# A tensor-product message kernel for a graph: three parts of the edges become two, and the other operand of the summing matmul becomes stationary

## The chip, the core and the metric

The kernel runs on one core of a Trainium2 chip. The core has five engines that each run their own list of instructions in order: TensorE (PE in the profile; its loads of the stationary operand are listed as PEld), VectorE (DVE), ScalarE (ACT), GpSimd (POOL) and SyncE (SP). Engines wait for each other through semaphores. Transfers are issued here by SP and, where rows are gathered or scattered by index, by POOL. The metric is the time of one execution in microseconds (us) on the device; lower is better.

## The reference

There are 10,000 nodes and 640,000 edges; each node has 64 channels of 4 components. What must be computed:

```python
R   = silu(edge_feat @ w_rad)                     # (E, 64): one factor per edge and channel
xs  = x[src]                                      # (E, 64, 4): gather by source node
tp  = einsum('eci,ef,ifo->eco', xs, Y, cg)        # Y: (E, 4), cg: (4, 4, 4)
msg = R[:, :, None] * tp
agg = segment_sum(msg, dst, N)                    # sum over edges by destination node
out = einsum('ncm,cd->ndm', agg, w_mix)           # (N, 64, 4)
```

`src` and `dst` are random, so edges come in no order.

## The kernel before

Because `cg` and `w_mix` are constants, the kernel sums, for every node, the products R * x[src] times each of the four components of Y, and applies `cg` and `w_mix` once per node at the end (`mix`). The sum over edges is a matmul over tiles of 128 edges, for which the edges must first stand together by destination. So the work has three kinds of steps.

**The first pass** (`pass1`) reads the edges of one part and sorts them into 18 groups of 576 destination nodes. An edge is a payload of 9 words (a key of source and destination, 4 of Y, 4 of edge_feat). It works in chunks of 12 tiles: `tables` counts and lays out up to 24 chunks at a time (NC is 24 in the lead-in, 14 later), `route` then builds, per chunk, a one-hot matrix (`oh`, L546 on DVE, L552 and L553 on ACT) and a spread payload (`X`, L537 on DVE), multiplies them (`pr`, L560), copies the result out (`rt`, L567 on ACT) and stores it by index (L571, POOL) to the tensor `grp`.

**The second pass** (`pass2`) does the same with one group after the other, in chunks of 11 tiles, and sorts a group into its 18 buckets of 32 nodes (tensor `bkt`). It loads the group's words into `Wt2` (L704; two buffers, the next group's load issued while the present group is laid out), and at the end loads the sorted payload back as `pay` (L732).

**The messages** (`messages`) run over units. A unit is one bucket of one part: 5 tiles in the first part, 6 in the second and in the third. For a unit POOL gathers the rows x[src] (L790, one indirect transfer per tile, `LG` = 6 units ahead, 8 buffers of `xg`); PE transposes the payload (L803); ACT copies it (L808); PE forms the radial product (`pre`, L813); ACT applies SiLU (L816); DVE builds the one-hot of the destination times Y (`spots`, L824 and L827, tile `S`), and multiplies x[src] by R in place (`products`, L834). Then `sums` (L844) adds up, per tile, one matmul with S as the stationary operand (128 edges x 128 columns: 32 nodes by 4) and the product as the moving one (256 columns), so that the bucket's sum stands with its nodes on the partitions. Each fp32 matmul shows in the profile as two passes.

The parts are not kept apart on the chip: a bucket's sum of the first part goes to the DRAM tensor `sums` (L868), the second part fetches it (L855, tile `old`), adds it on DVE while it takes the sum out of PSUM (L864) and stores it again, and the third does the same without storing. For the third, `flip` (L879) transposes the sum on PE, since `mix` (L903) needs the channels on the partitions, and `flipped` (L887, ACT) takes it out. The sums live in one PSUM bank of two halves, which are taken in turn by `sums` and by `flip`.

**Order.** The lead-in runs `pass1` of the first part while the DRAM tensors are cleared; there only SP's order is written by hand. Afterwards `groups` writes the order of PE, DVE and ACT by hand: one step in four of each unit (`quarters`) is followed by as many steps of the other generators as their due times ask for. `pass1` of a later part is spread so that it ends before the second-to-last group of the part ahead of it is through; `pass2` of a group is spread over the units of the group ahead of it. So while the first part's 313 units run, the second part is sorted for the first time; while the second part's 313 units run, the third; and while the third part's units run only the second pass is left beside them.

A few lines that a sentence can't say:

```python
SPLIT = ((0.3, (5,)), (0.355, (6,)), (0.345, (6,)))      # share of the edges, tiles of each unit of a bucket
quarters = (((index, LI), (gather, LG), (fetch, 4), (turn, 2), (sums, 0), (flip, -1), (silu, 1)),
            ((turned, 2), (spots, 1)), ((products, 1), (evict, 0), (flipped, -1)), ((radial, 2), (full, -1)))
```

`(f, a)` means that in step k the stage `f` of unit k + a is issued.

Of the kernel before, what the change touches and what calls it, by code (L numbers as in the profile page):

```python
# [18 lines left out]
F = mybir.dt.float32  # L19
# [6 lines left out]
P = 128  # L26
B = 18
W = 9
# [7 lines left out]
SPLIT = ((0.3, (5,)), (0.355, (6,)), (0.345, (6,)))  # L36
LG = 6
# [34 lines left out]
class Kernel:  # L72
    def __init__(self, ctx, tc, x, src, dst, Y, ef, w_rad, cg, w_mix, out):
# [56 lines left out]
        self.sums = self.dr.tile([self.NBK, NB * 4, 256], F, name="sums")  # L130
# [11 lines left out]
    def consts(self):  # L142
        nc, c = self.nc, self.cst

        def iota(name, pat, base=0, cm=0):
            t = c.tile([P] + [n for _, n in pat], F, name=name)
            nc.gpsimd.iota(t, pattern=pat, base=base, channel_multiplier=cm,
                           allow_small_or_imprecise_dtypes=True)
            return t

        self.zr = c.tile([16, max(self.p1.rw, self.p2.rw)], F, name="zr")
        nc.vector.memset(self.zr, 0.0)
# [10 lines left out]
        d = iota("dif", [[1, P]], cm=-1)  # L163
# [17 lines left out]
        self.L = c.tile([P, P], F, name="L")  # L181
        nc.vector.tensor_scalar(self.L, d, -0.5, None, op0=OP.is_le)
# [64 lines left out]
    def weights(self):  # L247
# [23 lines left out]
        wm2 = self.ph.tile([P, 2, 64], F, name="wm2", bufs=1)  # L271
# [10 lines left out]

        m = self.ph.tile([P, 4], F, name="io", bufs=1)
        nc.gpsimd.iota(m, pattern=[[-1, 4]], base=P, channel_multiplier=1, allow_small_or_imprecise_dtypes=True)
        mi = self.ph.tile([P, 4], I32, name="ioi", bufs=1)
        nc.vector.tensor_copy(mi, m)
        nc.vector.tensor_scalar(mi, mi, 3, None, op0=OP.bitwise_and)
        nc.vector.tensor_scalar(m, mi, 0.0, None, op0=OP.is_equal)
        self.wx = c.tile([P, 2, 64, 4], F, name="wx")
        for h in range(2):  # L290
            nc.vector.tensor_tensor(self.wx[:, h], wm2[:, h, :].unsqueeze(2).to_broadcast([P, 64, 4]),
                                    m.unsqueeze(1).to_broadcast([P, 64, 4]), op=OP.mult)
# [313 lines left out]
    def pass1(self, part, first):  # L606
# [12 lines left out]
        TB, DB, KB, SB = {}, {}, {}, {}  # L619
        nc.vector.memset(self.k1, 0.0)  # L620

        def front(b):

            o, e = cut[b] * T, min(cut[b + 1] * T, nt)
            m = e - o
            da = ph.tile([P, NC * T], I32, name="da", bufs=1)
            si = SB[b] = ph.tile([P, NC * T], I32, name="si", bufs=2)
            nc.sync.dma_start(da[:, :m], self.dst[:, lo + o:lo + e])
# [509 lines left out]
```

## Time and profile before

| | us |
|---|---|
| median of 3 runs (10965.9 to 10981.9) | 10973.87 |
| the profiled execution | 10891.28 |
| its span, from first to last instruction | 10889.4 |
| PE, PEld busy | 8139.3, 6372.5 |
| DVE busy | 6985.1 |
| POOL busy | 6023.7 |
| ACT busy | 4132.0 |
| mean granted TensorE clock | 0.833 |

The profile describes one execution. Busy times are by engine; a row of a group of instructions gives source line, engine, operation, output<-inputs, the count, the busy time in us and the mean duration of one in ns, and after a second bar the idle time of the engine just ahead of such instructions with what ended it ("issue" is idle time for which the profile shows no wait). A row of stretches gives start:end, length, the busy time of each engine with its count of instructions in brackets, the granted TensorE clock, the share of the DMA engines and GB/s. An engine at 75% is not necessarily the bound, and one at 64% is not necessarily free: the four engines hand each unit to one another several times.

### The profile page before, as it was taken

To read this page: it belongs to the slowest core of one execution; us is meant where nothing else is said; L and a number is where in the kernel's file an instruction comes from. 1 tells how busy PE (TensorE), PEld (TensorE's weight loads), DVE (VectorE), ACT (ScalarE), POOL (GpSimd) and SP (SyncE) were. 2 spreads that over 40 slices of the span, in tenths; PEclk is the share of its full clock that TensorE was granted. 3 is DMA by queue.
4 is the path that set the end of the run, shared out by engine and by line. 5 is a ranking of instruction groups with operands and counts; after the bars stand their busy time and mean duration, and the time that the engine had idled before them with its cause. 6 is when DMAs were issued, how large, how long until landed. Compare 5 with 4: busy or idle time off the path is not lost. (4 is left out here: it accounts for less than half of the span.)

```text
span 10889.4 us, 127350 instructions
## 1 busy us (share of the span) xinstructions
PE 8139.3 (75%) x41365; PEld 6372.5 (59%) x41365; DVE 6985.1 (64%) x12762; ACT 4132.0 (38%) x12102; POOL 6023.7 (55%) x6306
## 2 busy tenths in 40 slices
PE   5767777777777777777777777776778787777876
PEld 5656566656565565556555555555556565655654
DVE  6777667777666676666666666656656565555553
ACT  5654444444444343334334333332323232333321
POOL 1225555555555655555655555566666666666664
PEclk8878888888888887788888887887888888888887
DMA  8213233333333323333333333333333333333332
GB/s 156 77 42 93 83 87 96 90 91 93 92 86 90 101 83 97 102 96 101 109 101 98 106 102 95 99 109 110 106 103 100 104 99 104 99 103 100 101 103 73
DMA packets 696241, 1056.05 MB, mean 97 GB/s; under 512 B 251979, under 2 KB 500327, under 8 KB 695576
## 3 DMA queue, kind: packets, MB, share of 16 engines
q0 software_dynamic: 286560, 746.72, 24.0%
q1 hardware_dynamic: 406424, 293.41, 10.1%
q8 instruction: 328, 5.37, 0.2%
q10 hardware_dynamic: 2592, 7.78, 0.2%
q14 instruction: 337, 2.76, 0.1%
HBM read 856.49 MB, written 207.52 MB: 98 GB/s over the span
## 5 line engine op out<-in xcount | busy, mean ns | idle before, releaser
L790 POOL DMA_INDIRECT xg<-in_x_dram,sidx x5321 | 5052.4, 950 | 3151.5 <-issue 1427.6
L560 PE MATMUL pr<-X,oh 128*128 128x135 f32 (+1 forms) x21286 | 3147.2, 308 | 674.4 <-ACT rt L567 294.3
L560 PEld LDWEIGHTS pr<-X,oh 128*128 128x128 f32 x21286 | 2971.7, 218 | 1021.9 <-issue 505.5
L844 PE MATMUL G<-xg,S 128*128 128x256 f32 x10642 | 2958.3, 430 | 408.4 <-issue 265.2
L844 PEld LDWEIGHTS G<-xg,S 128*128 128x128 f32 x10642 | 2250.4, 219 | 829.2 <-issue 321.7
L537 DVE TENSOR_TENSOR X<-dv,Wt 128x1512 f32<-128x1512 f32 (+4 forms) x958 | 1600.8, 1671 | 774.5 <-remote 482.0
L834 DVE TENSOR_TENSOR xg<-xg,pre 128x1536 f32<-128x1536 f32 (+1 forms) x939 | 1556.9, 1658 | 501.3 <-ACT pre L816 365.6
L552 ACT ACTIVATE sq<-i,rowf 128x128 f32<-128x128 f32 x5658 | 1750.0, 392 | 9.5 <-DVE rowf L524 7.2
L813 PE MATMUL pre<-wr,sT 54*128 54x384 f32 (+1 forms) x1878 | 942.9, 585 | 419.4 <-ACT sT L808 370.1
L864 DVE TENSOR_TENSOR Gp<-old,G 128x256 f32<-128x256 f32 x626 | 262.3, 419 | 1541.1 <-remote 710.6
L553 ACT ACTIVATE oh<-sq,ones 128x768 f32<-128x768 f32 (+2 forms) x958 | 937.1, 978 | 204.6 <-remote 98.0
L571 POOL DMA_INDIRECT grp<-rt,idx x417 | 415.6, 997 | 948.9 <-ACT rt L567 508.8
L571 POOL DMA_INDIRECT bkt<-rt,idx x541 | 541.3, 1001 | 670.6 <-ACT rt L567 411.8
L827 DVE TENSOR_TENSOR S<-dv,pay 128x768 f32<-128x768 f32 (+1 forms) x939 | 857.5, 913 | 82.8 <-PE G L844 23.1
L816 ACT ACTIVATE pre<-pre 128x384 f32<-128x384 f32 (+1 forms) x939 | 429.1, 457 | 1222.8 <-PE pre L813 349.3
L546 DVE TENSOR_TENSOR oh<-dv,rowf 128x640 f32<-128x640 f32 (+2 forms) x922 | 800.7, 868 | 1.2 <-remote 1.2
L567 ACT ACTIVATE rt<-pr 128x135 f32<-128x135 f32 (+1 forms) x958 | 259.5, 271 | 1114.9 <-remote 620.5
L813 PEld LDWEIGHTS pre<-wr,sT 54*128 54x128 f32 (+1 forms) x1878 | 312.4, 207 | 623.9 <-ACT sT L808 417.1
L808 ACT ACTIVATE sT<-pre 54x128 f32<-54x128 f32 (+1 forms) x939 | 244.6, 261 | 698.2 <-remote 362.8
L507 ACT ACTIVATE pc<-pp 128x396 f32<-128x396 f32 (+3 forms) x506 | 244.0, 482 | 507.7 <-PE pp L499 218.4
L887 ACT ACTIVATE Gs<-G 128x256 f32<-128x256 f32 x313 | 118.9, 380 | 830.4 <-DVE Gp L864 590.9
L903 PE MATMUL po<-wf,Gs 128*128 128x256 f32 (+2 forms) x1392 | 338.5, 399 | 78.4 <-ACT Gs L887 63.7
(216 smaller groups left out, 5316.2 us busy)
## 6 DMA issues: line engine op xcount, KB each, us to landing
xg<-in_x_dram,sidx POOLq DMA_INDIRECT x5321
sums<-Gp SPq DMA_DIRECT2D x626, 128.0 KB
old<-sums SPq DMA_DIRECT2D x626, 128.0 KB
bkt<-z SPq DMA_DIRECT2D x24, 994.5 KB
pay<-bkt SPq DMA_DIRECT2D x34, 486.0 KB
ys<-in_Y_dram SPq DMA_DIRECT2D x104, 96.0 KB
es<-in_edge_feat_dram SPq DMA_DIRECT2D x104, 96.0 KB
out_dram<-ot SPq DMA_DIRECT2D x69, 128.0 KB
```

The lines of the kernel that those rows point to most:

```text
L537: nc.vector.tensor_tensor(X[:, :m, :].rearrange("p t (s w) -> p t s w", w=W), msk.unsqueeze(3).to_broadcast([P, m, ps.r, W]), QD[c // Q][1 ...
L546: nc.vector.tensor_tensor(oh[:, :v, :], self.v128.unsqueeze(1).to_broadcast([P, v, P]), row[:, o:o + v].unsqueeze(2).to_broadcast([P, v, P ...
L552: nc.scalar.activation(sq[:, u, :], self.i128, AF.Square, bias=to, scale=-1.0)
L553: nc.scalar.activation(oh[:, v:v + len(at), :], sq[:, :len(at), :], AF.Relu, bias=self.ones[:, 0:1], scale=-2.0)
L560: nc.tensor.matmul(pr[:, :ps.rw], oh[:, u, :], X[:, u, :], start=(u == 0), stop=(not on and u == m - 1))
L571: st = nc.gpsimd.indirect_dma_start(out=ps.dst, out_offset=bass.IndirectOffsetOnAxis(ap=idx[:, i:i + 1], axis=0), in_=RT.pop(c), in_offset ...
L790: nc.gpsimd.indirect_dma_start(out=xg[:, t, :], out_offset=None, in_=self.x, in_offset=bass.IndirectOffsetOnAxis(ap=si[:, u:u + 1], axis=0))
L813: nc.tensor.matmul(R, ST_.pop(k)[:ut * W], self.wr[:ut * W, :ut * 64], start=True, stop=True)
L816: nc.scalar.activation(RT[k], RT[k], AF.Silu)
L827: nc.vector.tensor_tensor(S[:, :ut], self.eq[:, :ut].unsqueeze(3).to_broadcast([P, ut, NB, 4]), pb[:, :, 1:5].unsqueeze(2).to_broadcast([P ...
L834: nc.vector.tensor_tensor(V, V, R.unsqueeze(3).to_broadcast([P, ut, 64, 4]), op=OP.mult)
L844: nc.tensor.matmul(G, S[:, t].rearrange("p n f -> p (n f)"), V[:, t].rearrange("p c i -> p (c i)"), start=(s + t == 0), stop=(last(k) and ...
```

## The change

The edges are cut into two parts instead of three: 30% with units of 5 tiles as before, and 70% with two units of 6 tiles for every bucket. The numbers that follow from the code: groups of the second part have 224 tiles (before 115 and 112 in the two parts that it replaces); chunks of the first pass stay 417 (124 + 293 instead of 124 + 148 + 145); chunks of the second pass become 523 (157 + 366) instead of 541 (157 + 192 + 192); units stay 939 and tiles 5,321. All 293 chunks of the second part's first pass now run beside the first part's 313 units, and beside the other 626 units runs the second pass alone. `tables` in the second pass lays out up to 21 chunks at once, not 11.

Further edits in the same change:

- `sums` takes the product R * x[src] as the stationary operand, in two halves of 128 columns, and S as the moving one: per tile two matmuls of 128 columns instead of one of 256. The sum then already has the channels on the partitions; `flip` and `flipped` go, and the last part's sum is written straight into the tile that `mix` reads.
- The sum of a bucket has one PSUM buffer, with no second half.
- A bucket of the second part is taken out of PSUM once in two units; `sums` is stored and fetched 313 times each instead of 626.
- The second pass has one `Wt2`, loaded when the group ahead is through, six steps ahead of its use.
- Gathers run 5 units ahead (6 buffers of `xg`) instead of 6 (8 buffers); `old` is fetched 3 units ahead with 3 buffers; `didx` has one buffer.
- In the lead-in, the destinations and sources of the next table are loaded when the present table starts (they were loaded when their own table started), and Y and edge_feat are loaded three blocks ahead instead of two. `weights` comes after the first 40 steps of the first pass. While the first group goes through the second pass ahead of the first unit, the first pass of the second part is stepped along with it.
- The constants that only the overflow code at the end needs (`wx`, `zr`, `L`) are built there.

```diff
-SPLIT = ((0.3, (5,)), (0.355, (6,)), (0.345, (6,)))
-LG = 6
+SPLIT = ((0.3, (5,)), (0.7, (6, 6)))
+LG = 5
...
+        def ends(b):
+            if b >= nb:
+                return
+            o, e = cut[b] * T, min(cut[b + 1] * T, nt)
+            da = AB[b] = ph.tile([P, NC * T], I32, name="da", bufs=1 + self.early)
+            si = SB[b] = ph.tile([P, NC * T], I32, name="si", bufs=2 + self.early)
+            nc.sync.dma_start(da[:, :e - o], self.dst[:, lo + o:lo + e])
+            nc.sync.dma_start(si[:, :e - o], self.src[:, lo + o:lo + e])
...
+            if b == 0 or not self.early:
+                ends(b)
             if b == 0:
-                load(0)
-                load(1)
+                for i in range(self.ahead):
+                    load(i)
+            if self.early:
+                ends(b + 1)
...
-            Wt = ph.tile([P, M, W], F, name="Wt2")
+            Wt = ph.tile([P, M, W], F, name="Wt2", bufs=1)
...
+        for k, g in self.segs:
+            nt = self.gt[k][g]
+            Wt = load(k, g)
+
+            for _ in range(6):
+                yield
...
-            nxt = load(*self.segs[i + 1]) if i + 1 < len(self.segs) and self.segs[i + 1][0] == k else None
...
-            xg = XG[k] = ph.tile([P, UT, 256], F, name="xg", bufs=LG + 2)
+            xg = XG[k] = ph.tile([P, UT, 256], F, name="xg", bufs=LG + 1)
...
             if s == 0:
-                GP[g, j] = half()
+                GP[g, j] = self.ps.tile([P, 2, NB, 4], F, name="G", tag="G", bufs=1)
...
             for t in range(ut):
-                nc.tensor.matmul(G, S[:, t].rearrange("p n f -> p (n f)"), V[:, t].rearrange("p c i -> p (c i)"),
-                                 start=(s + t == 0), stop=(last(k) and t == ut - 1), skip_group_check=True)
+                for h in range(2):
+                    nc.tensor.matmul(G[:, h].rearrange("p n f -> p (n f)"),
+                                     V[:, t, 32 * h:32 * h + 32, :].rearrange("p c i -> p (c i)"),
+                                     S[:, t].rearrange("p n f -> p (n f)"),
+                                     start=(s + t + h == 0), stop=(last(k) and t == ut - 1),
+                                     skip_group_check=True)
...
-        quarters = (((index, LI), (gather, LG), (fetch, 4), (turn, 2), (sums, 0), (flip, -1), (silu, 1)),
-                    ((turned, 2), (spots, 1)), ((products, 1), (evict, 0), (flipped, -1)), ((radial, 2), (full, -1)))
+        quarters = (((index, LI), (gather, LG), (fetch, 3), (turn, 2), (sums, 0), (silu, 1)), ((turned, 2), (spots, 1)),
+                    ((products, 1), (evict, 0)), ((radial, 2), (full, -1)))
...
-        while segs[0] not in self.pay:
-            next(sort)
...
+        self.done = -6
+        while segs[0] not in self.pay:
+            next(sort)
+            if later:
+                next(later[0][0])
...
-            self.lag = 2
+            self.lag, self.ahead, self.early = 2, 3, 1
...
-                self.weights()
                 for _ in range(40):
                     next(first, None)
+                self.weights()
...
-            self.lag = 1
+            self.lag, self.ahead, self.early = 1, 2, 0
...
+            self.overflow_consts()
```

106 lines of the change are left out of this document (42 added, 64 removed).

## The prediction

> **What bounds the kernel now.** I read the page's busy shares first, then the costliest groups, then stretches of the trace cut where the units change from one part to the next, and last the waits. The page and three of its groups:
>
> ```profile
> span 10889.4 us, 127350 instructions
> PE 8139.3 (75%) x41365; PEld 6372.5 (59%) x41365; DVE 6985.1 (64%) x12762; ACT 4132.0 (38%) x12102; POOL 6023.7 (55%) x6306
> L560 PE MATMUL pr<-X,oh 128*128 128x135 f32 (+1 forms) x21286 | 3147.2, 308 | 674.4 <-ACT rt L567 294.3
> L844 PE MATMUL G<-xg,S 128*128 128x256 f32 x10642 | 2958.3, 430 | 408.4 <-issue 265.2
> L864 DVE TENSOR_TENSOR Gp<-old,G 128x256 f32<-128x256 f32 x626 | 262.3, 419 | 1541.1 <-remote 710.6
> ```
>
> No engine is full. PE is nearest, with the sorting (L560) and the summing (L844) at 3 ms each. DVE stood idle 1541 us ahead of taking sums out of PSUM, which comes in its hand-written order before other work that could have run. The engines are bound to one another, so I price work by what a stretch of the kernel costs with more or less of it. The stretches (first, second and third part's units, then the densest 18 units), all engines, then the units (L834) and the sorting chunks (L537) in them:
>
> ```profile
> 815.00:4044.00 3229.00, 2466.87 (x12943) 1964.16 (x12943) 2213.26 (x4123) 1409.68 (x4192) 1815.27 (x1891) 0.84 0.32 90
> 4044.00:7678.00 3634.00, 2670.49 (x13360) 2080.10 (x13359) 2404.56 (x4249) 1326.13 (x3833) 2099.89 (x2194) 0.82 0.36 102
> 7678.00:10808.00 3130.00, 2434.18 (x11111) 1845.33 (x11111) 1760.60 (x2930) 918.29 (x2655) 1922.59 (x2019) 0.85 0.35 102
> ...
> 815.00:4044.00 3229.00, 463.31 (x313) 0.84 0.32 90
> 3816.00:4054.00 238.00, 26.62 (x18) 0.81 0.29 82
> ...
> 815.00:4044.00 3229.00, 550.66 (x324) 0.84 0.32 90
> 4044.00:7678.00 3634.00, 538.08 (x323) 0.82 0.36 102
> 7678.00:10808.00 3130.00, 271.42 (x171) 0.85 0.35 102
> 3816.00:4054.00 238.00, 45.46 (x27) 0.81 0.29 82
> ```
>
> A unit takes 10.3, 11.6 and 10.0 us in the three stretches (313 units each), with 1.04, 1.03 and 0.55 chunks beside it; in the dense window it takes 13.2 us with 1.5.
>
> **The change, part by part.** The sum is made against the profiled 10,891.28 us; the median of the runs, 10,973.87, stands 83 us above it.
>
> *1. Moving the first pass (the large term).* The second part's 293 chunks now all run beside the first part's units. From the code, some 10 of them run earlier, while the first group goes through the second pass; the rest, with the second pass's own, make about 449 chunks in the first stretch: 125 more than its 324. The other 626 units keep some 341 of 494: 153 fewer. What is a chunk worth? In the first stretch, from its mean to the dense window, (13.2 - 10.3) / (1.5 - 1.04) = 6.2 us. Between the second and third stretches, 504 us for 152 chunks, 3.3 us: a low end, since the third also pays for flips and mixing. With the flips and mixing all charged to it,
>
> ```profile
> L903 PE MATMUL po<-wf,Gs 128*128 128x256 f32 (+2 forms) x1392 | 338.5, 399 | 78.4 <-ACT Gs L887 63.7
> L879 PE MATMUL G<-ident,Gp 128*128 128x128 f32 x626 | 131.8, 290 | 28.8 <-issue 27.1 <-ACT Gs L887 1.0
> L887 ACT ACTIVATE Gs<-G 128x256 f32<-128x256 f32 x313 | 118.9, 380 | 830.4 <-DVE Gp L864 590.9
> ```
>
> it is (504 + 417 + 161) / 152 = 7.1, the high end. I take 5.7 for chunks that come in (near the dense window, the only row of that density) and 5.2, the middle, for those that go: +712 - 796 = **-84**. The ends: 6.2 in and 3.3 out, +270; 3.3 in and 7.1 out, -674. This difference of two large numbers carries most of the uncertainty.
>
> *2. Summing with the product stationary.* Four passes of 128 columns replace two of 256 per tile. Bursts at full clock:
>
> ```profile
> 6014.61 2.84 PE L560 MATMUL pr<-X,oh 128*128 128x126 f32 x24
> 9012.82 2.75 PE L844 MATMUL G<-xg,S 128*128 128x256 f32 x12
> 9016.56 2.82 PE L560 MATMUL pr<-X,oh 128*128 128x135 f32 x22
> ```
>
> Less one last pass's own length, a pass starts every 0.111 us at 126 columns, 0.121 at 135, 0.215 at 256; so 4 x 0.113 against 2 x 0.215, +22 ns a tile, +117 us for 5,321 tiles. PE is busy three quarters of the time, so **+90** on the path. Ends: 0 (hidden), and by busy and issue time together 4 x 0.161 - 2 x 0.303 = +39 ns, +207.
>
> *3. Flips and half of the takings-out go.* PE sheds 161 us, ACT 119, DVE half of L864's 262, and DVE's stalls there come half as often in the second part. Much of it lies beside other work: **-60** (0 to -300). The added strided read should cost L864 nothing, by L887, which reads rearranged data in 380 ns.
>
> *4. Tables.* The table layouts fall from 85 to 66.
>
> ```profile
> L469 DVE TENSOR_TENSOR rk<-rk,ov 128x11 f32<-128x11 f32 (+8 forms) x85 | 14.7, 173 | 2.7
> ```
>
> A second-pass table is 51 small DVE instructions in the code; at this row's 173 ns 8.8 us, so 19 fewer are 167 us of DVE. A third is taken as felt: **-50** (0 to -167).
>
> *5. One PSUM buffer for the sum.* The next bucket's first matmul now waits for the present bucket's copy. The third stretch already works so, since flips take every other half. There the wait was 1.7 us; in the first stretch, where ACT copies:
>
> ```profile
> PE G L844 <- DVE Gp L864: 1.7, 1, 1.7
> PE G L844 <- ACT Gp L866: 35.6, 17, 8.7
> ```
>
> **+30** (0 to +150: ACT gets busier there). Behind a waiting L844 on PE stand the radial product and the sorting chunks, and for these wait ACT and POOL.
>
> *6. Lead-in.*
>
> ```profile
> DVE key L635 <- DMA da<-in_dst_dram: 113.1, 5, 46.3
> 20.00:640.00 620.00, 452.04 (x3357) 394.12 (x3356) 475.88 (x911) 408.02 (x1221) 119.79 (x122) 0.88 0.46 98
> 126.50 51.03 SPq L243 DMA_DIRECT2D bkt<-z  x9
> 205.40 0.38 SPq L628 DMA_DIRECT2D da<-in_dst_dram  x1
> 160.00:200.00 40.00, 6.31 (x53) 5.82 (x52) 5.17 (x11) 9.37 (x31) 0.00 (x0) 0.64 1.13 163
> 680.00:720.00 40.00, 15.80 (x89) 10.01 (x87) 25.55 (x109) 8.43 (x31) 7.28 (x8) 0.62 0.09 24
> POOL grp L571 <- DMA grp<-z: 193.8, 23, 71.9
> ```
>
> DVE waits 113 us for five loads of destinations that stand on SP's queue behind clears of `bkt`. A table earlier they are there; the first of the five, at the start, stays: -90. Late next are the blocks of Y and edge_feat, now three ahead, and POOL's stores, which wait for clears (38 copied-out chunks can queue). The first pass stepped beside the first group's second pass fills half-idle engines (640 to 815) but makes that chain longer: +30. `weights` later and constants at the end: -5. Together **-65** (-130 to +25).
>
> *7. Shorter leads.* Six buffers of gathered rows, not eight:
>
> ```profile
> L834 DVE TENSOR_TENSOR xg<-xg,pre 128x1536 f32<-128x1536 f32 (+1 forms) x939 | 1556.9, 1658 | 501.3 <-ACT pre L816 365.6 <-issue 62.9 <-DMA xg<-in_x_dram,sidx 60.4
> DMA Wt<-grp: 2.9, 1
> ```
>
> DVE waits 60 us for gathers now; **+15** (0 to +60). On POOL's queue a gather now waits for the sum of one unit ago, not two, with stores behind it. The group load costs 0: six steps, more than a unit or 10 us, cover it (DVE waited 2.9 us once). On SP it now stands behind the reload `pay`, which waits for stores. With no cover, a load of 1 MB at the 100 GB/s of the stretches is 10 us, for 35 groups +350; that is not expected. Halving the traffic of `sums` is off the path: 0.
>
> Sum: -84 + 90 - 60 - 50 + 30 - 65 + 15 = **-124**. So 10,767 against the profile, 10,850 against the median.
>
> **The rivals.**
>
> *A, slower: the first stretch is crowded.* With 1.43 chunks a unit DVE has 1.4 times its sorting beside the same units, and PE's copies-out must keep pace. For it: the dense window, where each further chunk cost 6.2 us. Against: its DVE is busy 168 of 238 us, not full. If the chunks that leave were worth only 3.3, term 1 is +270: 11,204. It decides from 125 x in - 153 x out above +62: at 5.2 out, from 6.9 in; at 5.7 in, from 4.25 out.
>
> *B, slower: the second part's units keep the pace of the third's.*
>
> ```profile
> 8056.00:8241.00 185.00, 31.46 (x18) 0.85 0.35 101
> 8241.00:8425.00 184.00, 31.46 (x18) 0.85 0.35 102
> 10508.00:10667.00 159.00, 33.09 (x19) 0.83 0.39 111
> 6004.00:6006.00 2.00, 0.49 (x1) 0.49 (x2) 0.56 (x2) 0.82 (x4) 0.10 (x1) 0.58 0.01 2
> 6008.00:6010.00 2.00, 2.00 (x11) 2.00 (x11) 1.93 (x4) 1.12 (x2) 1.39 (x3) 0.50 0.29 77
> ```
>
> Group after group takes 184 to 185 us, 10.24 a unit, though nothing is full; with no sorting, 8.4. PE's clock drops to half after a gap and returns, so time that work gives back may be lost to the clock. At 10.24 for 590 units and 8.4 for the last 36, the two later stretches give 6,344 where the terms give about 5,950: 11,245. Against: less work has no reason to keep to one number. [...]
>
> *C, slower: doubled weight loads stand on the path.* With term 2 at +207 and term 5 at +150: 11,087. For it: L844's 265 us of issue idle, with twice the instructions to come. Against: L560's bursts, which already run one load per 128-column pass. [...]
>
> *D, faster: the later units free themselves.* With DVE stalling at half of the sums and both chunk prices near 7.1 out, 5.7 in: -374 in term 1: 10,560.
>
> *E: the lead-in gains nothing,* since the clears fill the DMA engines (share 1.13) and loads issued earlier land no earlier: 10,940.
>
> **How the numbers follow.** Forecast 0.42 (its own range 10,600 to 10,950), A 0.24, B 0.07, C 0.08, D 0.12, E 0.07. A measurement of this kernel tells about 0.2% (22 us) from no change. Faster: forecast, D and E less 0.06 at their edges, 0.55; slower: A, B, C and 0.01, 0.40; within 0.2%: 0.05. The range, 10,560 to 11,210, reaches over A's end and leaves out the tails of D and B.
>
> **What would show it.** Right: units of the first stretch near 13 us, of the rest near 9.4; L844 passes every 0.11 us in a burst; L635's wait for `da` below 30 us; waits of L844 for L866 under 100. Wrong: first-stretch units above 14, later ones above 9.9, or DVE waiting for `Wt`.

## The result: slower by 1.6%

The changed kernel takes 11,149.93 us (median; 11,126.92 to 11,152.0), beside 10,970.65 for the kernel before in the same measurement: ratio 1.0161, 95% interval 1.0146 to 1.0175. The forecast was 10,850, faster. The time lies inside the range given, 54 us under rival A's and 95 under rival B's, but the sign was wrong.

The profiled execution's span grew from 10,889.4 to 11,150.2 us, by 260.8, and so by 82 more than the medians: the profiled execution of the kernel before was 79 us faster than its median, that of the changed one 2 us slower. First the page of the changed kernel: span, busy times, and three groups (columns as before; `sums` is now L834, `products` L823, the taking-out L863).

```profile
span 11150.2 us, 143119 instructions
PE 8333.0 (75%) x50943; PEld 6955.9 (62%) x50943; DVE 6663.6 (60%) x11244; ACT 3967.9 (36%) x11564; POOL 6009.1 (54%) x6284
L834 PE MATMUL G<-S,xg 128*128 128x128 f32 x21284 | 3263.4, 316 | 842.2 <-issue 384.4
L823 DVE TENSOR_TENSOR xg<-xg,pre 128x1536 f32<-128x1536 f32 (+1 forms) x939 | 1557.6, 1659 | 1770.8 <-ACT pre L805 1589.4
L863 DVE TENSOR_TENSOR Gs<-old,G 128x256 f32<-128x256 f32 x313 | 131.3, 419 | 1349.1 <-PE G L834 568.2
```

DVE, ACT and POOL are less busy than before and PE is 194 us busier, yet the end came later: DVE's idle time ahead of the product rose from 501 to 1,771 us. Where in the kernel the time came, the stretches tell: the first 313 units, the second 313, the third 313; then the sorting chunks in them, by the tile `X` (the DVE count is the number of chunks).

```profile
768.00:4538.00 3770.00, 2956.87 (x19670) 2555.78 (x19670) 2736.91 (x5045) 1854.38 (x5482) 1947.99 (x2021) 0.87 0.28 81
4538.00:7884.00 3346.00, 2469.63 (x14028) 2002.16 (x14027) 1716.58 (x2498) 866.87 (x2463) 1967.79 (x2062) 0.80 0.30 90
7884.00:11090.00 3206.00, 2332.65 (x13108) 1904.90 (x13108) 1574.95 (x2225) 745.80 (x2123) 1912.57 (x2006) 0.80 0.31 91
...
768.00:4538.00 3770.00, 1512.28 (x10551) 1419.65 (x10550) 778.58 (x456) 0.87 0.28 81
4538.00:7884.00 3346.00, 602.64 (x3936) 535.75 (x3936) 307.62 (x185) 0.80 0.30 90
7884.00:11090.00 3206.00, 496.20 (x3232) 445.48 (x3232) 249.64 (x151) 0.80 0.31 91
```

The chunks of the kernel before (L537), cut at the same first products:

```profile
815.00:4054.00 3239.00, 554.10 (x326) 0.84 0.32 90
4054.00:7688.00 3634.00, 538.05 (x323) 0.82 0.36 102
7688.00:10807.00 3119.00, 268.01 (x169) 0.85 0.35 101
```

The change by stretch is so:

| | lead-in | first 313 units | second | third | tail |
|---|---|---|---|---|---|
| change, us | -47 | +531 | -288 | +87 | -21 |
| change in chunks | | +130 | -138 | -18 | |

If all of a stretch's change is put on its chunks, one that came in cost 531 / 130 = 4.1 us, and one that left gave back only 201 / 156 = 1.3 us. The 82 us by which the profiles differ more than the medians stand somewhere in this table; put wholly on the one or the other, they make the prices 3.5 in or 1.8 out. The waits that bear on the prediction's steps:

```profile
DVE xg L823 <- ACT pre L805: 1589.4, 243, 15.3
DVE xg L823 <- DMA xg<-in_x_dram,sidx: 145.1, 47, 8.9
DVE key L629 <- DMA da<-in_dst_dram: 42.3, 3, 30.0
...
PE G L834 <- DVE Gs L863: 369.7, 75, 9.4
PE G L834 <- ACT Gp L865: 70.9, 17, 11.5
```

The wait of DVE for SiLU's result is the large new one; that for loads of destinations fell from 113 to 42; PE now waits for DVE to take the last part's sum out of the one PSUM buffer.

**A difficulty with the measurement, told here because the ratios below can't be read without it.** The experiments ran on two chips on which the kernel before takes 8,749 to 8,774 us, not 10,971. The traces show two differences: the mean granted clock (0.833 in the first measurement, 0.901 in the experiments' trace of the same kernel), and that PE in the first measurement often issues its instructions singly, with no wait shown. PE's instructions of the changed kernel there (start, length, count; in brackets the idle time and what ended it):

```profile
9003.38 2.84 PE L834 MATMUL G<-S,xg 128*128 128x128 f32 x24
...
9011.36 0.48 PE L545 MATMUL pr<-X,oh 128*128 128x135 f32 x2 [0.23 <-issue]
9012.07 0.28 PE L545 MATMUL pr<-X,oh 128*128 128x135 f32 x1 [0.23 <-issue]
...
9014.91 0.39 PE L545 MATMUL pr<-X,oh 128*128 128x135 f32 x1 [1.14 <-issue]
9016.34 0.38 PE L545 MATMUL pr<-X,oh 128*128 128x135 f32 x1 [1.04 <-issue]
```

and the same kernel's same work on a chip of the experiments:

```profile
7003.38 2.84 PE L834 MATMUL G<-S,xg 128*128 128x128 f32 x24
...
7015.01 2.97 PE L545 MATMUL pr<-X,oh 128*128 128x135 f32 x22
```

The bursts of 24 are equal to the hundredth (2.84 us); but in the first, groups of a few passes start 0.7 or 1.4 us apart. Taking the matmuls and the loads of PE in one list by their starts, and counting those that start 0.66 to 0.74 or 1.36 to 1.44 us after the one ahead: 996 before and 1,504 after in the first measurement (836 and 1,197 us), 123 and 121 (89 and 100 us) in the experiments' traces of the same two kernels. What makes PE issue so was not found. Each ratio below therefore compares runs on one chip. What can be carried over is bounded by this: the change's effect there, +3.4%, splits among the stretches much as in the first measurement (the first experiment shows it), but what holds the later units is another thing.

### The profile page after: what moved, and what is told of

It reads as the page before. It is cut to its first block, busy times and chain, and to the rows that moved or that the text cites. A ratio compares the mean times of both kernels' runs of the same rounds, so it can differ in the third digit from the quotient of the medians.

```text
span 11150.2 us, 143119 instructions
## 1 busy us (share of the span) xinstructions
PE 8333.0 (75%) x50943; PEld 6955.9 (62%) x50943; DVE 6663.6 (60%) x11244; ACT 3967.9 (36%) x11564; POOL 6009.1 (54%) x6284
## 3 DMA queue, kind: packets, MB, share of 16 engines
q10 hardware_dynamic: 2592, 7.78, 0.2%
## 5 line engine op out<-in xcount | busy, mean ns | idle before, releaser
L834 PE MATMUL G<-S,xg 128*128 128x128 f32 x21284 | 3263.4, 316 | 842.2 <-issue 384.4
L834 PEld LDWEIGHTS G<-S,xg 128*128 128x128 f32 x21284 | 3098.2, 230 | 962.1 <-issue 474.6
L545 PE MATMUL pr<-X,oh 128*128 128x135 f32 (+1 forms) x21180 | 3066.5, 299 | 831.1 <-issue 552.8
L545 PEld LDWEIGHTS pr<-X,oh 128*128 128x128 f32 x21180 | 2828.5, 208 | 1079.4 <-issue 751.9
L823 DVE TENSOR_TENSOR xg<-xg,pre 128x1536 f32<-128x1536 f32 (+1 forms) x939 | 1557.6, 1659 | 1770.8 <-ACT pre L805 1589.4
L522 DVE TENSOR_TENSOR X<-dv,Wt 128x1485 f32<-128x1485 f32 (+4 forms) x940 | 1590.3, 1692 | 399.0 <-remote 214.0
L537 ACT ACTIVATE sq<-i,rowf 128x128 f32<-128x128 f32 x5605 | 1733.8, 393 | 37.1 <-DVE rowf L509 35.9
L538 ACT ACTIVATE oh<-sq,ones 128x896 f32<-128x896 f32 (+2 forms) x940 | 926.4, 986 | 84.7 <-remote 35.6
L863 DVE TENSOR_TENSOR Gs<-old,G 128x256 f32<-128x256 f32 x313 | 131.3, 419 | 1349.1 <-PE G L834 568.2
L531 DVE TENSOR_TENSOR oh<-dv,rowf 128x640 f32<-128x640 f32 (+3 forms) x922 | 800.3, 868 | 0.0
L792 PEld LDWEIGHTS pre<-ident,pay 128*54 128x54 f32 (+1 forms) x939 | 108.6, 116 | 541.9 <-issue 314.3
L882 PEld LDWEIGHTS po<-wf,Gs 128*128 128x128 f32 (+2 forms) x1392 | 291.3, 215 | 138.5 <-issue 69.0
```

Of the source, the lines that this page charges most:

```text
L522: nc.vector.tensor_tensor(X[:, :m, :].rearrange("p t (s w) -> p t s w", w=W), msk.unsqueeze(3).to_broadcast([P, m, ps.r, W]), QD[c // Q][1 ...
L531: nc.vector.tensor_tensor(oh[:, :v, :], self.v128.unsqueeze(1).to_broadcast([P, v, P]), row[:, o:o + v].unsqueeze(2).to_broadcast([P, v, P ...
L537: nc.scalar.activation(sq[:, u, :], self.i128, AF.Square, bias=to, scale=-1.0)
L538: nc.scalar.activation(oh[:, v:v + len(at), :], sq[:, :len(at), :], AF.Relu, bias=self.ones[:, 0:1], scale=-2.0)
L545: nc.tensor.matmul(pr[:, :ps.rw], oh[:, u, :], X[:, u, :], start=(u == 0), stop=(not on and u == m - 1))
L823: nc.vector.tensor_tensor(V, V, R.unsqueeze(3).to_broadcast([P, ut, 64, 4]), op=OP.mult)
```

## The experiments

Stretches are cut at the product of units 1, 314, 627 and 939. All times in us, one chip's kernel before beside each.

| run | median | before | ratio (95%) | lead-in | first | second | third | tail |
|---|---|---|---|---|---|---|---|---|
| before_again | 8748.83 | 8752.98 | 0.9997 (0.9987-1.0008) | 762 | 2518 | 2834 | 2560 | 84 |
| after_again | 9047.68 | 8751.44 | 1.0337 (1.0320-1.0355) | 738 | 3102 | 2597 | 2558 | 63 |
| b_prod | 8765.27 | 8751.05 | 1.0014 (1.0005-1.0024) | 762 | 2519 | 2851 | 2552 | 79 |
| b_lead5 | 8755.21 | 8751.05 | 1.0008 (0.9999-1.0018) | 761 | 2520 | 2837 | 2570 | 83 |
| b_leadin | 8719.07 | 8751.44 | 0.9960 (0.9946-0.9974) | 730 | 2515 | 2834 | 2554 | 84 |
| b_onewt | 8831.49 | 8751.44 | 1.0092 (1.0075-1.0109) | 764 | 2578 | 2855 | 2549 | 84 |
| a_three | 8812.75 | 8751.05 | 1.0073 (1.0056-1.0090) | 747 | 2552 | 2874 | 2558 | 77 |
| a_onehot | 9038.10 | 8751.05 | 1.0331 (1.0314-1.0349) | 735 | 3091 | 2592 | 2550 | 63 |
| a_g2 | 9059.89 | 8774.38 | 1.0326 (1.0309-1.0343) | 752 | 3101 | 2588 | 2553 | 63 |
| a_act7 | 9058.53 | 8774.38 | 1.0323 (1.0306-1.0341) | 757 | 3097 | 2588 | 2552 | 62 |
| a_gath5 | 8253.63 | 8751.44 | 0.9430 (0.9414-0.9446) | 737 | 3101 | 2201 | 2155 | 60 |
| b_gath | 8464.59 | 8752.98 | 0.9671 (0.9655-0.9687) | 762 | 2540 | 2738 | 2332 | 83 |
| a_pe | 8974.09 | 8752.98 | 1.0251 (1.0233-1.0268) | 741 | 3028 | 2595 | 2560 | 63 |
| a_dve | 8943.58 | 8752.98 | 1.0216 (1.0199-1.0233) | 737 | 3001 | 2588 | 2553 | 63 |
| a_half | 8802.42 | 8774.38 | 1.0031 (1.0020-1.0043) | 1141 | (626 units) 4145 | | (626) 3426 | 96 |
| b_half5 | 8771.39 | 8774.38 | 0.9997 (0.9987-1.0006) | 1102 | (626 units) 4143 | | (626) 3427 | 98 |

### The two kernels again (before_again, after_again)

No edit.

> The changed kernel itself, on the chip of these experiments, where the kernel before takes 8,751 us and PE issues without the stalls of the first profile. If the split's own cost is the cause (first stretch bound by DVE and PE, later stretches kept by POOL's gathers), 9,000 to 9,080 us: the first stretch 9.6 to 10.1 us a unit, the later ones 8.2. If PE's slow issue with a fifth more instructions made the first comparison, 8,740 to 8,850 us.

> The kernel before, unchanged, for a trace of it on the chip of the experiments. If GpSimd's transfers pace it (1.25 us for each transfer of 128 rows, 1.3 for each chunk's store), its 313 units of a part take 5 x 1.25 + 1.04 x 1.3 = 7.6, 6 x 1.25 + 1.03 x 1.3 = 8.8 and 6 x 1.25 + 0.55 x 1.3 = 8.2 us; the run with shorter leads took 8.05, 9.06 and 8.21, so 2,520, 2,840 and 2,565 us are expected. If GpSimd does not pace it, its own waits for other engines ahead of gathers are several hundred us in each stretch.

Before, by stretches (all engines), and then the chunks (L537):

```profile
762.00:3280.00 2518.00, 2218.68 (x12985) 1793.25 (x12986) 2217.51 (x4132) 1415.97 (x4211) 1819.85 (x1888) 0.92 0.40 116
3280.00:6113.00 2833.00, 2396.84 (x13374) 1900.02 (x13373) 2394.82 (x4254) 1328.37 (x3825) 2103.35 (x2188) 0.90 0.45 131
6113.00:8673.00 2560.00, 2212.80 (x11063) 1715.28 (x11061) 1745.73 (x2917) 902.25 (x2642) 1940.09 (x2028) 0.91 0.43 124
...
762.00:3280.00 2518.00, 554.12 (x326) 0.92 0.40 116
3280.00:6113.00 2833.00, 538.09 (x323) 0.90 0.45 131
6113.00:8673.00 2560.00, 268.01 (x169) 0.91 0.43 124
```

and after:

```profile
738.00:3840.00 3102.00, 2708.07 (x19706) 2368.22 (x19705) 2741.86 (x5045) 1859.48 (x5484) 1941.11 (x2006) 0.93 0.34 99
3840.00:6436.00 2596.00, 2183.49 (x13988) 1860.82 (x13988) 1718.66 (x2498) 886.58 (x2459) 1969.48 (x2056) 0.89 0.39 115
6436.00:8994.00 2558.00, 2100.43 (x13124) 1787.35 (x13122) 1577.55 (x2224) 765.39 (x2124) 1938.57 (x2026) 0.88 0.39 115
```

By stretch the change is -24, +584, -237, -2, -21: 4.5 us for each of 130 chunks that came in (4.1 in the first measurement), 1.5 for each of 156 that left (1.3). So prices near those of the first measurement come back here. POOL's waits in before's third stretch (total, times, longest):

```profile
POOL xg L790 <- issue: 474.4, 1556, 0.3
POOL bkt L571 <- issue: 49.7, 163, 0.3
POOL xg L790 <- PE G L844: 29.9, 98, 0.3
```

POOL is busy 1,940 us and spends 474 + 50 in pauses of 0.3 us between transfers that no wait explains, and 30 in 98 pauses of the same length that are put down to PE: 2,494 of 2,560. The rest are pauses as short, put down to other engines: with every pause of up to 0.32 us counted, whatever it is put down to, the sum is 2,557, and no pause is longer. POOL is full there, at 76% busy. In the first stretch the same sum, with 0.30 us of each longer wait in it, is 2,395 of 2,518, with 60 longer waits, and in the second 2,771 of 2,834, with 27. So it has room in the first stretch, and little in the second.

### Which part of the change costs: b_prod, b_lead5, b_leadin, b_onewt, a_three

*b_prod*: the kernel before with the product stationary, one PSUM buffer and no flips.

```diff
-                nc.tensor.matmul(G, S[:, t].rearrange("p n f -> p (n f)"), V[:, t].rearrange("p c i -> p (c i)"),
...
+                for h in range(2):
+                    nc.tensor.matmul(G[:, h].rearrange("p n f -> p (n f)"),
+                                     V[:, t, 32 * h:32 * h + 32, :].rearrange("p c i -> p (c i)"),
+                                     S[:, t].rearrange("p n f -> p (n f)"),
...
-        def flip(k):
...
-        def flipped(k):
```

> The kernel before, with one edit: the product R * x[src] is the stationary operand of the sum, in two halves of 128 columns, with one PSUM buffer and without flips. Three theories of the 180 us that the change lost. V (the doubled passes and the single PSUM buffer cost the later units their gain): 11,120 to 11,220 us. L (the shorter lead of the gathers costs it) and S (the split into two parts costs it): within 60 us of 10,971, as terms 2, 3 and 5 of the prediction sum to +60.

Measured: 1.0014, some 14 us. The second stretch grew by 17, the third fell by 8 with the flips gone.

*b_lead5*: gathers 5 ahead, 6 buffers.

```diff
-LG = 6
+LG = 5
...
-            xg = XG[k] = ph.tile([P, UT, 256], F, name="xg", bufs=LG + 2)
+            xg = XG[k] = ph.tile([P, UT, 256], F, name="xg", bufs=LG + 1)
```

> The kernel before, with gathers 5 units ahead and 6 buffers instead of 6 units and 8 buffers. L: 11,070 to 11,170 us, with DVE's waits for gathered rows well over the 60 us of before. V and S: within 30 us of 10,971.

Measured: 1.0008, not told apart from none. DVE's waits for gathered rows did rise, from 117 us in before_again to 475, but other waits fell by as much.

*b_leadin*: the kernel before with the change's lead-in alone (destinations and sources a table ahead, blocks three ahead, `weights` after 40 steps, the next part's first pass stepped beside the first group).

```diff
+            if self.early:
+                ends(b + 1)
...
-            self.lag = 2
+            self.lag, self.ahead, self.early = 2, 3, 1
...
+        while segs[0] not in self.pay:
+            next(sort)
+            if later:
+                next(later[0][0])
```

> The kernel before with the lead-in of the change alone: next table's destinations and sources early, Y and edge_feat three blocks ahead, weights later, the next part's first pass stepped beside the first group's second pass. The prediction's term 6: -65 us, with the first unit's product 65 to 100 us earlier. Rival (the clears fill the DMA engines and the added chain delays the first unit): within 20 us of the kernel before, or above it.

Measured: 0.9960, 32 us, all of it in the lead-in (762 to 730). This kernel beats both. DVE's wait for destinations fell by 18 us only, from 79.7 to 61.2.

*b_onewt*: the kernel before with one `Wt2`, loaded when the group ahead is through.

```diff
-            Wt = ph.tile([P, M, W], F, name="Wt2")
+            Wt = ph.tile([P, M, W], F, name="Wt2", bufs=1)
...
+            for _ in range(6):
+                yield
...
-        return (self.gt[k][g] + 23) // 24 + 12 + self.p2.carry + 6 + self.ls + HEAVY * nch
+        return (self.gt[k][g] + 23) // 24 + 18 + self.p2.carry + 6 + self.ls + HEAVY * nch
```

> The kernel before with one buffer for the second pass's words, loaded when the group ahead is through and used six steps later. The prediction's term 7: within 20 us of the kernel before. Theory W (the late load starves the second pass, and explains the +62 us of the three-part variant of the changed kernel): +40 to +80 us.

Measured: 1.0092, some 80 us, of which 60 in the first stretch. It isn't a wait for the load. The largest that any engine waits for `Wt` there, and for `old`, which stands on SP's queue behind such loads:

```profile
POOL grp L571 <- DMA Wt<-grp: 8.8, 3, 5.9
DVE dg L721 <- DMA Wt<-grp: 5.5, 2, 3.0
...
DVE Gp L864 <- DMA old<-sums: 129.8, 18, 18.2
```

In the kernel before on such a chip `old` is waited for 142.2 us, so that isn't new. The edit also puts six empty steps into each group and moves the due times that `groups` works to; that this order costs the 60 us is argued, not shown.

*a_three*: the whole change with three parts.

```diff
-SPLIT = ((0.3, (5,)), (0.7, (6, 6)))
+SPLIT = ((0.3, (5,)), (0.355, (6,)), (0.345, (6,)))
```

> The changed kernel with the three parts of before (30, 35.5 and 34.5%), all else as changed. S: 10,850 to 10,950 us, since only the lead-in's gain and the small terms are left. V: 11,050 to 11,200 us. L: 11,000 to 11,150 us.

Measured: 1.0073. The four single parts above sum to 0.14 + 0.08 - 0.40 + 0.92 = +0.74%, the same. The cut into two parts takes the rest, from 1.0073 to 1.0337: against a_three the first stretch costs 550 more, and the two later give back 277 + 0. As all else is equal between these two, this is the cleanest price of the move: 550 for 138 chunks in, 4.0 each, and 277 for 156 out, 1.8 each.

### Is it the summing or its buffer: a_onehot, a_g2

*a_onehot*: the change with the one-hot stationary again, flips and two halves.

```diff
-                    nc.tensor.matmul(G[:, h].rearrange("p n f -> p (n f)"),
-                                     V[:, t, 32 * h:32 * h + 32, :].rearrange("p c i -> p (c i)"),
...
+                nc.tensor.matmul(G, S[:, t].rearrange("p n f -> p (n f)"), V[:, t].rearrange("p c i -> p (c i)"),
...
+        def flip(k):
...
+        def flipped(k):
```

> The changed kernel with the one-hot stationary again, the bank of two halves and the flips, all else as changed. V: 10,900 to 10,990 us, and L834's two bursts of waits (for DVE's copy 370 us, for issue 384 us) fall to those of before (71 and 265). S and L: 11,100 to 11,200 us.

Its sums are not the reference's. The flips write to the other half of the bank between a bucket's two units; whether that is the cause, no run shows. Measured: 1.0331, beside 1.0337 of the change. *a_g2*: the change with two PSUM halves in turn.

```diff
+        bank = self.ps.tile([P, 2, 2, NB, 4], F, name="G", tag="G", bufs=1)
...
-                GP[g, j] = self.ps.tile([P, 2, NB, 4], F, name="G", tag="G", bufs=1)
+                GP[g, j] = bank[:, next(turns)]
```

> The changed kernel with the sum of a bucket in two halves of its PSUM bank in turn. The prediction's term 5: 0 to 30 us less here (the one-buffer variant of the kernel before lost 14 us in all). Rival (the single buffer, whose wait was 370 us in the first profile, carries the loss): 100 us less or more.

Measured: 1.0326, no stretch moved by more than 9 us but for a lead-in 14 longer. On these chips neither the passes nor the single buffer cost anything that can be seen in the changed kernel. It is no test of the first measurement: there PE waited 369.7 us for the single buffer to be taken out by DVE, while in after_again the same wait is 1.8 us.

### What the later units rest on: a_gath5, b_gath

*a_gath5*: five gathers instead of six in the later units.

```diff
-            for t in range(ut):
+            for t in range(min(ut, 5)):
```

> The changed kernel with 5 gathers instead of 6 in each of the 626 later units; the sixth tile takes the first one's rows, so its part of the sum is wrong, while PE, DVE and ACT do as much as before. Theory F (POOL's gathers, 1.25 us each back to back, are the floor of the later units: 6 x 1.25 + 0.58 x 1.3 = 8.26 us): 400 to 750 us below the changed kernel, 7.0 to 7.5 us a unit. Rival N (the later units are held by the chain between PE, DVE and ACT): within 100 us of it.

```profile
3837.00:6038.00 2201.00, 2018.01 (x14011) 1714.13 (x14010) 1760.12 (x2812) 879.58 (x2463) 1669.34 (x1746) 0.95 0.40 117
6038.00:8193.00 2155.00, 1931.86 (x13122) 1635.58 (x13120) 1619.12 (x2536) 757.79 (x2123) 1632.01 (x1711) 0.94 0.40 118
```

The two later stretches lost 396 and 403 us. A gather takes 0.95 us with 0.3 between two, so 313 fewer are 391: all of it came through, 799 us for both stretches where 750 was expected at most. POOL's rows of the changed kernel (after_again; columns: count, busy, mean, idle ahead and what ended it), in a window of 312 later units, 6,440 to 9,000:

```profile
L779 POOL DMA_INDIRECT xg<-in_x_dram,sidx x1867 | 1778.4, 953 | 569.2 <-issue 509.5 <-DMA bkt<-rt,idx 21.3 <-PE pre L802 10.4
L556 POOL DMA_INDIRECT bkt<-rt,idx x156 | 157.3, 1008 | 47.5 <-issue 43.3 <-ACT oh L538 1.8 <-ACT sT L797 1.8
```

Busy time and idle time of an engine always add up to the window, so what tells is that none of this idle time is a wait: in the window, and in both later stretches, no pause of POOL is longer than 0.32 us. So on these chips the later units stand on POOL's gathers: 6 x 1.25 + 0.54 x 1.3 = 8.2 us a unit, and in this window DVE waited 796 us for them. A chunk that leaves such a stretch gives back its one store on POOL, 1.3 us, and not its work on PE, DVE and ACT.

*b_gath*: the kernel before with one gather less in each unit.

```diff
-            for t in range(ut):
+            for t in range(ut - 1):
```

> The kernel before with one gather less in each unit (the last tile takes the rows of the unit's first, so that tile's messages are not the reference's; the product is split in two instructions, 0.3 us more of VectorE a unit). If GpSimd's transfers pace the kernel before in all three stretches, each loses near 1 us a unit: 313 units in about 2,250, 2,480 and 2,200 us, in all 7,700 to 7,950 us. If VectorE and TensorE already stand close behind (0.88 and less busy), the first two stretches give only half of that, 8,150 to 8,350.

```profile
762.00:3302.00 2540.00, 2225.76 (x12983) 1793.55 (x12983) 2258.96 (x4444) 1417.17 (x4210) 1523.94 (x1579) 0.92 0.34 99
3302.00:6040.00 2738.00, 2393.10 (x13378) 1895.61 (x13377) 2439.68 (x4569) 1330.36 (x3825) 1819.88 (x1889) 0.92 0.42 121
6040.00:8372.00 2332.00, 2150.89 (x11057) 1676.99 (x11057) 1788.18 (x3230) 902.11 (x2642) 1631.46 (x1705) 0.94 0.40 118
```

The three stretches moved by +22, -96 and -228 us, so 8,465: neither expectation held. The second instruction of the product cost DVE 41 us in the first stretch, 0.13 us a unit, not 0.3. Of the 391 us of gathers, 228 came through in the third stretch, where PE (2,151 of 2,332 us busy) stands close behind, 96 in the second and none in the first. It fits the change's second stretch: with 138 chunks POOL lost as many stores of 1.3 us, 179, and the 63 us of longer waits that it had, and 237 us came back, down to the floor of the gathers, 8.3 us a unit; the third was at the floor already and gave 2.

### What the crowded first stretch rests on: a_act7, a_pe, a_dve

*a_act7*: 7 of 12 one-hot tiles of a chunk on ACT, not 6.

```diff
-        self.p1 = Pass(T, r, max(map(max, self.gt)) * P // r, 6, False)
+        self.p1 = Pass(T, r, max(map(max, self.gt)) * P // r, 7, False)
```

> The changed kernel with 7 instead of 6 of the 12 one-hot tiles of a first-pass chunk built on ACT, 5 on DVE: 0.16 us of DVE a chunk moves to ACT (0.39 us and more there). If DVE bounds the first stretch: 30 to 60 us less in it (9,000 us). If PE does: within 15 us of the changed kernel.

Measured: first stretch 3,097 beside 3,102, as was expected if DVE isn't the bound. *a_pe*: less summing on PE in the first part.

```diff
-                for h in range(2):
+                for h in range(1 if g[0] == 0 and t else 2):
```

> The changed kernel with the second half of the channels summed for the first tile of a unit alone in the first part's units (the rest of that half is left out of the sum): 8 passes of 0.113 us, 0.9 us of TensorE, less in each of the first 313 units, nothing else changed. If TensorE (0.87 busy) paces the first stretch: 3,100 falls to about 2,820, in all 8,770. If VectorE or the handing to and fro does: 3,060 to 3,100, in all about 9,030.

*a_dve*: a smaller product on DVE in the first part.

```diff
+            if units[k][0][0] == 0:
+                V, R = V[:, :, :24], R[:, :, :24]
```

> The changed kernel with the product R * x[src] formed for 24 of the 64 channels in the first part's units (the other channels go into the sum without R): about 0.85 us of VectorE less in each of the first 313 units, nothing else changed. If VectorE (0.89 busy) paces the first stretch: 3,100 falls to about 2,840, in all 8,790. If TensorE does: 3,060 to 3,100. If both have to fall together, neither this run nor the one with less TensorE moves it by more than 100 us.

The first stretch of a_pe:

```profile
741.00:3769.00 3028.00, 2501.12 (x17196) 2140.29 (x17196) 2732.75 (x5044) 1861.85 (x5484) 1938.34 (x2004) 0.90 0.35 101
```

and of a_dve:

```profile
737.00:3738.00 3001.00, 2660.40 (x19701) 2326.18 (x19701) 2484.02 (x5044) 1855.36 (x5484) 1935.96 (x2005) 0.95 0.35 102
```

PE's busy time fell by 207 us and the stretch by 74; DVE's by 258 and the stretch by 101. So neither paces it alone, and neither of a_pe's expected times (2,820, or 3,060 to 3,100) came: PE and DVE are busy for 0.87 and 0.88 of the stretch, and some 0.4 of what is taken from either comes through. That they hold each other up by handing the work to and fro is the likely reading; a kernel with less of both was not run. POOL has room there: 2,006 transfers at 1.25 us are 2,508 of 3,102.

### The cut at half: a_half, b_half5

*a_half*: the change with 53% and 47%, units of 5 + 4 and 4 + 4 tiles.

```diff
-SPLIT = ((0.3, (5,)), (0.7, (6, 6)))
+SPLIT = ((0.53, (5, 4)), (0.47, (4, 4)))
```

> The changed kernel with the edges cut in the middle: 53% with units of 5 + 4 tiles and 47% with 4 + 4 (17 tiles a bucket as before, 1,252 units), all else as changed. Theory S1 (two parts lose because the 30 to 70 cut crowds 293 first-pass chunks beside 313 small units, where DVE and PE are full, while POOL's gathers keep the rest): with some 200 chunks beside 626 units POOL is the floor throughout, 5,321 x 1.25 + 940 x 1.3 = 7,870 plus lead-in and end of 800: 8,680 to 8,850 us. Rival S2 (two parts as such lose: larger tables, one buffer of words): above 8,950 us.

Measured: 1.0031 beside 1.0337. The lead-in is 403 us longer, with more of the first pass in it; then 464 chunks stand beside 626 units, 0.74 each, where the change has 1.46. Both stretches stand at POOL's transfers: 4.5 x 1.25 + 0.74 x 1.3 = 6.6 us a unit (measured 6.62), and 4 x 1.25 + 0.36 x 1.3 = 5.5 (measured 5.47, with 224 chunks). So on these chips it is the crowding that cost, not the number of parts. *b_half5*: the kernel before with this cut, the product stationary, the new lead-in, gathers 5 ahead and two `Wt2`.

```diff
-SPLIT = ((0.3, (5,)), (0.355, (6,)), (0.345, (6,)))
-LG = 6
+SPLIT = ((0.53, (5, 4)), (0.47, (4, 4)))
+LG = 5
```

> The kernel before with the product stationary, the lead-in of the change, gathers 5 units ahead and the same cut in the middle, but two buffers of words in the second pass. S1: 8,640 to 8,730 us, below the kernel before (8,751) and below its lead-in variant (8,719) or level with it. S2: above 8,800 us.

Measured: 0.9997, level with before, and not below it as was expected. Beside a_half only the lead-in's time differs, by 39 us; with both kernels' stretches at POOL's floor, the second `Wt2` gave nothing.

## Why the prediction was wrong, step by step

**1. Moving the first pass: the step that failed.** It put 5.7 us on each chunk in and 5.2 on each chunk out, -84. Measured in the first measurement: 4.1 in (130 chunks, +531, less than the +712 set) and 1.3 out (156, -201, where -796 was set). The inflow was over-priced; the outflow was four times over-priced, and its lowest end, 3.3, was still too high. The fault lies in taking one price from differences between stretches: that supposes that the later stretches shorten with the work in them. On the experiments' chips they have a floor that sorting hardly touches, the gathers of the unit itself (a_gath5), and the third stretch was at that floor before the change (POOL's waits in before_again). In the first measurement POOL wasn't full: its gathers waited for PE,

```profile
POOL xg L779 <- PE G L834: 1440.4, 330, 13.7
POOL xg L779 <- issue: 1413.0, 4606, 4.5
```

where before it was 666.5 us for the sums and 355.1 for the flips. There the later units have a steady pace too. The first row is 288 of the changed kernel's units, from unit 314 on (the next 288 take the same 3,068 us); the second is units 627 to 896 of the kernel before. Below them are PE's rows for the sums in these windows (after, before):

```profile
4538.00:7606.00 3068.00, 502.99 (x288) 0.80 0.31 90
7688.00:10455.00 2767.00, 471.93 (x270) 0.85 0.35 101
...
L834 PE MATMUL G<-S,xg 128*128 128x128 f32 x13818 | 2177.3, 320 | 593.3 <-issue 337.6 <-DVE Gs L863 239.8 <-DMA xg<-in_x_dram,sidx 7.0
L844 PE MATMUL G<-xg,S 128*128 128x256 f32 x3240 | 907.8, 429 | 169.2 <-issue 148.8 <-ACT Gs L887 8.8 <-DMA xg<-in_x_dram,sidx 6.9
```

That is 10.65 us a unit, with 21 chunks beside every 36 units; the kernel before took 10.25, with 11 chunks beside 18, which is a little more sorting, and with the flips. So two things are missing from the gain. At the old third's pace the second stretch would have taken 313 x 10.25 = 3,208 us, 426 less than its 3,634, and the third, with 18 chunks fewer, little less than before: about half of the 796 set. And some 0.4 us a unit more, which the chunks can't explain, goes with the rest of the change. PE's row for the sums takes 4.8 us of a unit, busy and idle, where it took 4.0 and the flips 0.5; 0.42 of it is the wait for DVE's taking-out from the one buffer, which the row of before doesn't show. PE's single issues, counted as above, rose too, from 281 to 490 us in the second stretch and from 289 to 437 in the third. Which of these holds the pace is open: no run shows it. In the experiments' traces of the two kernels PE issued so 123 and 121 times, and after_again's wait for the buffer is 1.8 us. That both measurements lose nearly the same, 330 and 345 us over the three stretches, may be chance.

**2, 3 and 5. Product stationary, flips, one buffer.** Set at +90, -60, +30; b_prod, which holds all but the halved takings-out, shows about +14 on the experiments' chips, and a_onehot and a_g2 show nothing. The passes came every (2.84 - 0.28) / 23 = 0.111 us, as worked out. The wait for the single buffer came, 369.7 us, but from DVE's taking-out in the second part, where the prediction looked at ACT's in the first (70.9, under its 100); a_g2 shows that on the experiments' chips, where that wait is missing, a second half gives nothing. What these terms cost in the first measurement is the open part of step 1.

**4. Tables.** They went from 85 to 66, as said (`rk` stands 66 times), and DVE shed 321 us in all. What that is worth on the path was not tried by itself.

**6. Lead-in.** Set at -65; -47 in the first measurement, and -32 in b_leadin. The sign was right, the cause only in part: the wait for destinations fell by 71 us in the first measurement, to 42 where below 30 was said (beside the first load, 30.0 us, two short ones are left), but by 18 in b_leadin, where 32 us were gained.

**7. Shorter leads.** The gathers were set at +15; b_lead5 shows 1.0008, although DVE's waits for them grew. The one `Wt2` was set at 0 with the argument that six steps cover the load. They do (in b_onewt DVE waited 5.5 us for it in all); yet b_onewt costs 80 us. A price was put on the load and none on the steps and due times that came with it.

**The rivals.** A had the right sign and named the crowding that a_half shows; that its time came so near is luck, since two errors offset: a chunk in was to cost 6.2 us and cost 4.1, a chunk out was to give back 3.3 and gave 1.3. B describes best what happened: the later units kept near the pace of the old third stretch, 10.7 and 10.2 us where 10.24 was set (forecast: 9.4). The reason that it named, time lost to PE's clock, no run shows. The trace of the kernel before has such a drop: a granted clock of 0.50 from 6,006 to 6,010 us, after PE had been busy for 1.71 of the 6 us ahead, and 1.00 from 6,012 to 6,018. The mean clock of the two later stretches fell too, from 0.82 and 0.85 to 0.80 and 0.80; but on the experiments' chips, where POOL's transfers hold the changed kernel's later units, it fell likewise, from 0.90 and 0.91 to 0.89 and 0.88. Windows of 2,600 us in the first measurement, with the products in them:

```profile
5000.00:7600.00 2600.00, 424.63 (x243) 0.81 0.30 90
8100.00:10700.00 2600.00, 427.37 (x245) 0.80 0.30 90
```

are 10.70 and 10.61 us a unit; the later stretches take 8.3 and 8.2 in the experiments' trace of the same kernel, so the units keep to no one number. C falls with the bursts (a pass every 0.111 us) and, on the experiments' chips, with a_onehot (1.0331 beside 1.0337). In the first measurement it isn't excluded: PE's time for the sums grew there from 2,958 to 3,263 us, and the issue idle ahead of them from 265 to 384. D needed an outflow price of 7.1. E is refuted by b_leadin.

**What would show it.** Passes every 0.11 us: right. Waits for L865 under 100: right. First-stretch units near 13: 12.04, not above the 14 set as wrong. Later units near 9.4, wrong above 9.9: 10.5, and this is the sign that the prediction itself had named.

## What to carry to other kernels

Before work is moved from one stretch to another, ask of each stretch what would be left as its floor: on the experiments' chips the units' own gathers, so that the crowded stretch paid 4.5 us for each chunk and the emptied ones paid 1.5 back. A price per piece of work from the difference of two stretches holds at most between them (there 1.8 us a chunk between the second and the third, and the second gave back 1.7), not below the emptier one. And the engine that issues the transfers was full at 76% busy (POOL, 1,940 of 2,560 us): its pauses of 0.30 us between them belong to its time.

## What the hardware showed that was not expected

- The same kernel takes 10,971 us in one measurement and 8,749 to 8,774 in others (the kernel before), with PE's bursts (12 passes for the sums: 2.75 and 2.76 us), a gather (0.95) and a product of 6 tiles (1.75) of equal duration. The traces differ in PE's single issues 0.7 or 1.4 us apart (996 against 123) and in the mean granted clock (0.833 against 0.901). The cause is open, and a per cent of one measurement need not be that of another: this change costs 1.6% in the one and 3.4% in the other.
- A gather of 128 rows by index occupies POOL for 0.95 us and is followed by a pause of 0.30 us: in the first measurement's two traces none of 5,321 is followed by a shorter one, and with nothing to wait for it is never longer than 0.32 us (the later stretches of after_again).
- In the crowded first stretch, no one of two engines at 0.87 and 0.88 busy sets the pace: 207 us off PE gave 74, 258 off DVE gave 101.
